# Another order for the loads of the first batch in a fused retention and mixer kernel, and halved copies of its half chunk

## Chip, core and metric

The kernel runs on one core of one Trainium2 chip. The metric is the device time in microseconds (us) from start to end of one execution; the time of a kernel is the median of its runs.

## What is computed

The inputs q, k, v have 8 batches, 8 heads, 576 positions and 64 features per head, float32. Stage one is a retention (attention without softmax and with a decay), stage two a low-rank mixing over the positions and then a two-layer network of width 2048:

```python
scores = scale * np.matmul(q, k.transpose(0, 1, 3, 2))
gamma = 1.0 - 2.0 ** (-5.0 - np.arange(H, dtype=np.float32))
Dmat = np.where(rel >= 0, gamma[:, None, None] ** rel[None, :, :], 0.0)
ret = np.matmul(scores * Dmat[None], v)          # then heads side by side: x
h = x.transpose(0, 2, 1) @ U @ V                 # U: 576 x 32, V: 32 x 576
u = x + h.transpose(0, 2, 1)
out = u + np.maximum(u @ w_ch1, 0.0) @ w_ch2     # 512 -> 2048 -> 512
```

## The kernel before, in words

Positions are cut into chunks of 128; a batch has four and a half of them, and two batches share one chunk (number 4, `XC`), each with one half of its 64 + 64 rows. I call that part of batch 0 or 1 the half chunk. The decay is split into a factor on q and one on v, so that within a chunk the scores are only masked (the product is called SC, the masked result `ret`), and what earlier chunks contribute is a running state S = k'v, kept in PSUM (ST) and multiplied by q (QS). RV multiplies `ret` by v into PSUM; the sum is copied to the tile x (L759 and L757 for pairs of chunks, L932 for a half chunk). MA multiplies U by x to a 32-row result a; `build` transposes x through the identity and adds V times a on PE, and copies the result to uT (L1041, L1043). Y1 is the first layer (weights w1, 64 products for each group of four chunks, ReLU on ScalarE), Y2 the second, added to u and stored.

Batches 0 and 1 have a path of their own, since nothing else can cover their loads. q of batch 0 comes in two transfers, k and v as pairs of chunks (`load_pair`, names k0, v0 for chunks 0 and 1, k2, v2 for chunks 2 and 3), the half chunk by `load` as kA, qA, vA for batch 0 and kB, qB, vB for batch 1. U comes in two transfers (lu), V in one (lv, L1164), which reads V's 32 rows four times over, to fill 128 partitions. The weights come in 16 transfers w0 to w15. All of these are issued on the SP queue. Casting and scaling are spread over GpSimd (POOL), VectorE (DVE) and ScalarE (ACT): k casts at L521 and L523, v scaled at L526 for pairs and at L472 for a half chunk, q of the half chunk at L478, U at L1169, V at L1173, V's second copy at L1177, weights at L1197 and L1215.

The order in which each engine works is fixed when the kernel is built. Every piece of work is an `Op` with engine, an assumed duration, dependences, buffers taken and given back, and a priority; `Plan.run` simulates the engines with these durations and picks, for each engine, the next op by time and priority. Its transfers share one ring: a transfer is done `work` after the one before it, plus `DMA_LAT`, and SP does not issue more than `DMA_AHEAD` ahead of the ring. The order of the first 40 or so loads is not left to it: a line of names is written out by hand and each load is put after the one before it (L1329 to L1331):

```python
line = [ld["q4a", 0], ld["q4", 0]] + [load_op(x) for x in ("k0 k2 v0 kA qA v2 vA lu lv w0 w1" + " " + "w2 w3 w4 w5 w6 w7 w8 w9 q4 w10 w11 kB k5 qB vB v5 k7 w12 w13 w14 w15 lub v7").split()]
for a, b in zip(line, line[1:]):
    b.after.append(a)
```

Before the first Y1 the planned gaps on PE are filled with products of a zero tile (`zeros`, from L1348), which have no use but to keep PE at work. The first three output tiles of Y1 are done in two halves, so that they can start when two of the four uT pieces and the first weight cast are ready.

Of the kernel before, what the change touches and what calls it, by code (L numbers as in the profile page):

```python
# [28 lines left out]
class Plan:  # L29

    LAT = {"PE": 230.0, "ACT": 80.0, "DVE": 80.0, "POOL": 90.0}
    LOOK = {"DVE": 150.0, "ACT": 150.0}
    DMA_LAT = 1700.0
    DMA_AHEAD = 4500.0

    def __init__(self):
        self.ops = []
# [21 lines left out]
    def run(self, hint=None):  # L59
        size = {name: len(x) for name, x in self.pools.items()}  # L60
        self.pools = {name: [0.0] * n for name, n in size.items()}
        self.held, self.spans, since = {}, {}, {}
        for o in self.ops:
            o.users, o.ready = [], 0.0
        urgent = {"DVE": [], "ACT": []}
        if hint:
            for o in self.ops:
                if o.prio < 0 and o.engs[0][0] in urgent and len(o.engs) == 1:
                    urgent[o.engs[0][0]].append(o)
        engines = ("PE", "ACT", "DVE", "POOL", "SP")  # L70
        free = dict.fromkeys(engines, 0.0)
        ring = 0.0
        avail = {e: [] for e in engines}
        for o in self.ops:
            o.n_wait = len(o.deps) + len(o.after)
            for d in o.deps + o.after:
                d.users.append(o)

        def add(o):
            pe = o.engs[0][0] == "PE"  # L80
            o.ready = max([d.end if pe and d.engs[0][0] == "PE" else d.vis for d in o.deps]
                          + [d.end for d in o.after], default=0.0)
            for e, dur in o.engs:
                avail[e].append((o, dur))

        for o in self.ops:
            if not o.n_wait:
                add(o)
        order = []
        left = len(self.ops)  # L90
        INF = float("inf")

        self.n_rel, self.last = {}, {}
        for o in self.ops:
            for x in o.rel:
                self.n_rel[x] = self.n_rel.get(x, 0) + 1
        for pool in self.line:
            self.line[pool] = sorted(
                (o for o in self.ops if any(x[0] == pool for x in o.acq)), key=lambda o: o.prio
            )  # L100

        def earliest(o):
            t = o.ready
            for pool, key in o.acq:
                if pool in self.line and self.line[pool][0] is not o:
                    return INF
                n = sum(x[0] == pool for x in o.acq)
                t = max(t, sorted(self.pools[pool])[n - 1])
            return t

        wary = bool(hint)
        while left:
            best = None
            for e in engines:
                base = free[e]
                if e == "SP":
                    base = max(base, ring - self.DMA_AHEAD)
                te = INF
                cand = []
                for o, dur in avail[e]:  # L120
                    t = max(base, earliest(o))
                    if t == INF:
                        continue
                    if wary and o.prio > 0 and any(
                        t < (max(hint[h], h.ready)) < t + dur - 150.0 for h in urgent.get(e, ())
                    ):
                        continue
                    cand.append((t, o, dur))
                    te = min(te, t)
                if te == INF:  # L130
# [12 lines left out]
            _, e, o, dur, t = best  # L143
            for en, _ in o.engs:
                avail[en] = [x for x in avail[en] if x[0] is not o]
            o.start, o.end = t, t + dur
            if hint and e in urgent and o in urgent[e]:
                urgent[e].remove(o)
            free[e] = o.end
            if e == "SP":  # L150
                ring = max(ring, t + 700.0) + o.work
                o.vis = ring + self.DMA_LAT
            elif o.work:
                ring = max(ring, o.end + 500.0) + o.work
                o.vis = ring + self.DMA_LAT
            else:
                o.vis = o.end + self.LAT[e]
            for pool, key in o.acq:
                if pool in self.line:
                    self.line[pool].pop(0)  # L160
                s = self.pools[pool]
                i = min(range(len(s)), key=lambda i: s[i])
                s[i] = INF
                self.held[pool, key] = i
                since[pool, key] = o.start
            for x in o.rel:
# [12 lines left out]
        return order  # L179
# [3 lines left out]
def kernel(  # L183
# [11 lines left out]
    nc = tc.nc  # L195
# [74 lines left out]
    def slot(pool, key):  # L270
        return pl.held[pool, key]
# [75 lines left out]
    def DMA(issue, work, fn, **kw):  # L347
        return pl.op("SP", issue, fn, work=work, **kw)
# [4 lines left out]
    def load_q4(par, prio):  # L353
# [5 lines left out]
        for n, hs in enumerate(halves):  # L359
            def fn(e, hs=hs):  # L360
# [2 lines left out]
                    out=q4.rearrange("p (h x) -> p h x", h=H)[:, hs, :],  # L363
                    in_=q[par, hs, t0:t0 + 4 * P, :].rearrange("h (p r) d -> p h (r d)", r=4),
                )
            gots.append(DMA(600.0, 3300.0 if par else (1500.0, 2400.0)[1 - n], fn, prio=prio + 0.01 * n,
                            acq=[] if n else keys))
        ld["q4", par] = gots[-1]
        ld["q4a", par] = gots[0]
# [57 lines left out]
    def load(p, c, prio, early=False, b=None):  # L427
# [17 lines left out]
        for n, (j, dram) in enumerate(((1, k), (0, q), (2, v))):  # L445

            def fn(e, j=j, dram=dram):
                f = at(j)
                for rw, bb, t0 in pts:
# [1 line left out]
                        out=f[rw, :, :],  # L451
                        in_=dram[bb, :, t0:t0 + rw.stop - rw.start, :].rearrange("h s d -> s h d"),
                    ))
            got[j] = DMA(480.0 if len(pts) == 1 else 900.0, 1220.0 if b is None else 1000.0, fn,
                         prio=prio + (0.0, 0.01, 0.5)[n], acq=[] if j == 2 else [home[j]],
                         after=[] if j == 1 else [got[1]])
            if p:
# [430 lines left out]
    def RV(p, c, prio, q_done=True, b=None, in_sc=False):  # L888
# [33 lines left out]
        def ev(e):  # L922
# [5 lines left out]
                ),  # L928
                op=ALU.mult,
            )  # L930
        def ev_x(e):
            nc.scalar.activation(out=xs[slot(*xk)][rows].rearrange("p hp hl d -> p hl hp d"),  # L932
                                 in_=po[rows, :, 0:NHP * D].rearrange("p hl (hp d) -> p hl hp d", d=D),
                                 func=AF.Copy)
        if b is None:
            st["x", kb] = [pl.op("DVE", 700.0, ev, [o], prio, rel=[pk])]
        else:
            st["x", kb] = [pl.op("ACT", 610.0, ev_x, [o], prio, rel=[pk])]
        if b is not None:
            st.setdefault(("x", c), []).extend(st["x", kb])  # L940

# [209 lines left out]
    def load_uv():  # L1151
# [11 lines left out]
        def fv(e):  # L1163
            nc.sync.dma_start(out=vst, in_=moe_V[None, :, :].to_broadcast([4, R, S]))  # L1164

        ld["lu"] = DMA(1200.0, 500.0, fu, prio=-999.0, after=[ld["consts"]])
        ld["lub"] = DMA(1200.0, 500.0, fub, prio=-999.0)
        ld["lv"] = DMA(500.0, 800.0, fv, prio=-999.0)
        ld["U"] = pl.op("POOL", 250.0, lambda e: gp.tensor_copy(out=UU[:, 0:5, :], in_=ust[:, 0:5, :]),  # L1169
                        [ld["lu"]], -970.0)  # L1170
        ld["UB"] = pl.op("POOL", 250.0, lambda e: gp.tensor_copy(out=UU[:, 5:10, :], in_=ust[:, 5:10, :]),
# [8 lines left out]
    def load_w(prio):  # L1180
        ld["lw"] = []
        for fb in range(4):
            ld["w1", fb] = []
            for hc in range(2):
                key = ("wst", ("w1", fb, hc))

                def fn(e, fb=fb, hc=hc, key=key):
# [3 lines left out]
                            "(c p) n -> p c n", p=P),  # L1191
                    ))
                o = DMA(450.0, 1400.0 + 350.0 * (fb < 2), fn, prio=prio + fb + hc * 0.1, acq=[key])
                ld["lw"].append(o)

                def cast(e, fb=fb, hc=hc, key=key):
# [4 lines left out]
        for fb in range(4):  # L1201
            ld["w2", fb] = []
            for hf in range(2):
# [3 lines left out]
                def fn(e, f=f, key=key):  # L1207
                    sent.append(nc.sync.dma_start(
                        out=wst[slot(*key)].rearrange("p (f d) -> p f d", d=dm),
                        in_=moe_w_ch2[f * P:(f + 2) * P, :].rearrange("(f p) d -> p f d", p=P)))  # L1210
                o = DMA(450.0, 1400.0, fn, prio=prio + 10 + fb + hf * 0.1, acq=[key])
                ld["lw"].append(o)

                def cast(e, f=f, key=key):
# [9 lines left out]
    def batch0():  # L1224
# [2 lines left out]
        load_q4(0, base - 3.0)  # L1227
        t_q4(0, base - 2.0, 10.0)
        for i in range(2):
            load_pair(0, i, base + 20 * i, scaled=(2, 2)[i])  # L1230
        load(0, XC, base + 40.0, early=True, b=0)
        for r in range(4):
            t_pe(0, r, base + 10 * r + 2)
            SC_pair(0, r, base + 10 * r + 3, home=("po", "sc")[r % 2])
        t_pe(0, XC, base + 42.0, b=0)
        SC(0, XC, base + 43.0, with_q=False, b=0, apart="sc" == "big")
        sp = -4.0
        ST_four([base + sp, base + sp + 2, base + sp + 4, base + 5.0, base + 52.7])
        for i in range(2):
# [83 lines left out]
    def load_op(x):  # L1323
# [2 lines left out]
        if x[0] == "w":  # L1326
            return ld["lw"][int(x[1:])]
        return ld["q4", 1] if x == "q4" else L(x)[0]
    line = [ld["q4a", 0], ld["q4", 0]] + [load_op(x) for x in ("k0 k2 v0 kA qA v2 vA lu lv w0 w1" + " " + "w2 w3 w4 w5 w6 w7 w8 w9 q4 w10 w11 kB k5 qB vB v5 k7 w12 w13 w14 w15 lub v7").split()]  # L1329
    for a, b in zip(line, line[1:]):  # L1330
        b.after.append(a)  # L1331
    def shift(g):
# [67 lines left out]
```

## Time and profile before

| | |
|---|---|
| median of 6 runs | 337.85 us (336.59 to 340.07) |
| the profiled execution | 336.59 us, of which the span of the profile is 334.4 us |
| PE busy | 326.2 us of the span, 98% |
| DVE, ACT, POOL busy | 151.4, 134.6, 84.2 us |
| queue of SP's transfers (q1) | 47.12 MB, 69.3% of the 16 engines' span |
| first Y1 product | at 24.33 us |
| PE busy from 60 to 140 us | 79.99 of 80 us |

All times in the views count from the start of the span. A line of the chain of waits has start, length and what the time went to; in the lists in order of time a line has start, length, engine, line of the kernel, operation, output and input, count, and in square brackets the idle time before it with what ended it. A row of stretches gives, after the stretch's bounds, its length and the busy time of PE, PE's weight loads, DVE, ACT and POOL with their instruction counts, then the granted PE clock, the share of time in which the DMA engines were busy and the GB/s that they moved.

The loads up to w0 were issued at these times: k0 and k2 from 1.84, v0 3.46, kA 6.08, qA 7.81, v2 8.71, vA 9.57, U 11.46 and 12.28, V 13.51, w0 and w1 from 14.21 us.

### The profile page before, as it was taken

The page shows a single profiled execution, that of the slowest core. Times are in us where ns is not written, and L with a number is a line of the kernel's source. Part 1 is how long each engine was busy: PE and PEld are TensorE (multiplying, and loading weights), DVE is VectorE, ACT ScalarE, POOL GpSimd, SP SyncE. Part 2 cuts the span into 40 slices and gives each one's busy share as a digit, 9 for nine tenths or more (in the row PEclk, how much of TensorE's full clock was granted, in tenths as well). Part 3 has the DMA queues.
Part 4 walks back from the last instruction along what each step waited for, and adds up shares of the span by engine and source line. Part 5 has one row for each costly group of instructions (what it writes and reads, how often), then busy time and mean ns, then how long its engine had stood idle before and what let it go on. Part 6 is the DMA issues. An engine that isn't in the chain of part 4 may idle for free.

```text
span 334.4 us, 6464 instructions
## 1 busy us (share of the span) xinstructions
PE 326.2 (98%) x2656; PEld 161.0 (48%) x2656; DVE 151.4 (45%) x238; ACT 134.6 (40%) x240; POOL 84.2 (25%) x116
## 2 busy tenths in 40 slices
PE   8989999999999999999999999999999999999995
PEld 3554445555545544544454455444544444444442
DVE  5842275786555537664476538533633020020011
ACT  4756564478303650265114521364035206404600
POOL 7567456522321312131122113200100010010010
PEclk9999999999999999999999999999999999999999
DMA  8999999999999999999999989913110320011012
GB/s 238 228 305 359 296 247 301 266 244 187 192 257 207 226 179 213 233 221 205 185 235 227 188 186 235 217 37 49 63 65 16 71 89 31 0 65 63 0 51 76
DMA packets 145169, 56.44 MB, mean 169 GB/s; under 512 B 128244, under 2 KB 138484, under 8 KB 145140
## 3 DMA queue, kind: packets, MB, share of 16 engines
q1 hardware_dynamic: 142420, 47.12, 69.3%
q0 software_dynamic: 2720, 8.92, 7.7%
q8 instruction: 21, 0.34, 0.4%
q14 instruction: 8, 0.07, 0.1%
HBM read 37.14 MB, written 9.44 MB: 139 GB/s over the span
## 4 chain that ended last, share of the span: by engine, by line
PE 86%; DMA 8%; DVE 3%; POOL 1%; SPq 1%; issue 0%; DVEq 0%
PE ps_big_t L326 72%; DMA st_st<-in_k_dram 5%; PE ps_o L326 5%; PE ps_s L326 5%; PE ps_sc L326 3%; DMA vst<-in_moe_V_dram 2%; PE ps_big_t L566 1%; DVE ret_t L713 1%; DVE ret_t L857 1%; DVE o_sb L1127 0%; SPq L1156 0%; SPq L450 0%; POOL w_sb L1197 0%; PE ps_sc L401 0%; DVE qkv_t L468 0%
## 5 line engine op out<-in xcount | busy, mean ns | idle before, releaser
L326 PE MATMUL ps_big_t<-uT_t,w_sb 128*128 128x512 bf16 x576 | 133.7, 379 | 0.5 <-POOL w_sb L1197 0.5
L326 PE MATMUL ps_big_t<-w_sb,y_t 128*128 128x512 bf16 x576 | 133.3, 379 | 0.1
L1060 ACT ACTIVATE y_t<-ps_big_t 128x512 bf16<-128x512 f32 x144 | 85.8, 597 | 94.3 <-PE ps_big_t L326 94.1
L326 PEld LDWEIGHTS <-w_sb 128*128 128x128 bf16 x576 | 53.9, 98 | 62.1 <-POOL w_sb L1197 1.0
L326 PEld LDWEIGHTS <-y_t 128*128 128x128 bf16 x576 | 53.8, 98 | 60.9 <-issue 0.8
L1127 DVE TENSOR_TENSOR o_sb<-ps_big_t,u_t 128x512 f32<-128x512 f32 x36 | 24.7, 689 | 87.8 <-PE ps_big_t L326 87.7
L1134 POOL DMA_DIRECT2D out_dram<-o_sb x34 | 19.3, 567 | 161.6 <-DVE o_sb L1127 161.4
L472 POOL TENSOR_TENSOR qkv_t<-st_st,vscale 128x512 bf16<-128x512 f32 (+1 forms) x28 | 29.2, 1041 | 57.3 <-DMA st_st<-in_v_dram 43.1
L857 DVE TENSOR_TENSOR ret_t<-ps_sc,tri 128x1024 bf16<-128x1024 f32 x24 | 29.3, 1221 | 20.3 <-PE ps_sc L326 20.1
L798 ACT ACTIVATE s_sb<-ps_s 128x512 bf16<-128x512 f32 x22 | 13.1, 596 | 56.5 <-PE ps_s L326 56.4
L923 DVE TENSOR_TENSOR x_t<-ps_o,qscale 128x512 bf16<-128x512 f32 x27 | 18.6, 687 | 15.4 <-PE ps_o L326 15.3
L991 DVE TENSOR_TENSOR u_t<-ps_s,x_t 128x512 bf16<-128x512 f32 x20 | 13.8, 690 | 21.1 <-PE ps_s L326 21.0
L326 PEld LDWEIGHTS <-qkT_t 64*128 64x128 bf16 (+3 forms) x612 | 15.3, 99 | 11.0 <-issue 8.0
L326 PEld LDWEIGHTS <-ret_t 128*128 128x128 bf16 (+2 forms) x384 | 12.5, 99 | 8.2 <-issue 0.8
L468 DVE CAST qkv_t<-st_st 128x512 bf16<-128x512 f32 x27 | 13.6, 503 | 3.5 <-DMA st_st<-in_k_dram 3.5
L468 DVE CAST qkv_t<-q_st 128x512 bf16<-128x512 f32 x27 | 13.9, 516 | 2.3 <-DMA q_st<-in_q_dram 2.3
L326 PE MATMUL ps_o<-qkv_t,ret_t 128*128 128x64 bf16 (+2 forms) x344 | 13.2, 193 | 0.6 <-DVE ret_t L713 0.4
L326 PE MATMUL ps_sc<-qkT_t 64*128 64x128 bf16 (+2 forms) x336 | 13.3, 215 | 0.4 <-DVE ret_t L857 0.4
L326 PE MATMUL ps_s<-qkv_t 64*64 64x64 bf16 (+3 forms) x200 | 12.8, 207 | 0.5 <-issue 0.3
L326 PEld LDWEIGHTS <-qkv_t 64*64 64x64 bf16 (+3 forms) x232 | 9.9, 104 | 6.5 <-issue 2.8
L991 DVE TENSOR_TENSOR u_t<-ps_o,x_t 128x512 bf16<-128x512 f32 x16 | 10.9, 683 | 3.4 <-PE ps_o L326 3.3
L575 ACT ACTIVATE qkT_t<-ps_big_t 128x512 bf16<-128x512 bf16 (+1 forms) x21 | 10.9, 555 | 2.0 <-PE ps_big_t L566 1.7
(101 smaller groups left out, 178.7 us busy)
## 6 DMA issues: line engine op xcount, KB each, us to landing
out_dram<-o_sb POOLq DMA_DIRECT2D x34, 256.0 KB, 3.2
st_st<-in_k_dram SPq DMA_DIRECT2D x24, 256.0 KB, 4.6
q_st<-in_q_dram SPq DMA_DIRECT2D x24, 256.0 KB, 4.6
st_st<-in_v_dram SPq DMA_DIRECT2D x24, 256.0 KB, 5.2
y_t<-in_moe_w_ch_dram SPq DMA_DIRECT2D x10, 512.0 KB, 9.9
wst_t<-in_moe_w_ch_dram SPq DMA_DIRECT2D x6, 512.0 KB, 6.6
st_st<-in_k_dram SPq DMA_DIRECT2D x4, 512.0 KB, 7.5
st_st<-in_v_dram SPq DMA_DIRECT2D x4, 512.0 KB, 7.8
```

The lines of the kernel that those rows point to most:

```text
L326: nc.tensor.matmul(*a, skip_group_check=True, **kw)
L468: nc.vector.tensor_copy(**args)
L472: eng.tensor_tensor(out=qkv[slot(*qk)][rows, 2, :, :], in0=at(2)[rows], in1=vscale[rows, c, :, None].to_broadcast([rows.stop - rows.start, ...
L566: nc.tensor.transpose(pst()[:, hp, :], t[rows, j, 2 * hp:2 * hp + 2, :].rearrange("p h d -> p (h d)"), ident[rows, rows],)
L575: nc.scalar.activation(func=AF.Copy, **args)
L798: nc.scalar.activation(out=s_sb[slot(*sk)], in_=ps_s.rearrange("p (a b) -> p a b", b=P), func=AF.Copy)
L857: nc.vector.tensor_tensor(out=ret[slot(*rk)][rows, hl, :, 0:n], in0=bank(hl.start)[rows, None, :, 0:n] if apart else ps_sc[rows, hl, :, 0: ...
L923: nc.vector.tensor_tensor(out=xs[slot(*xk)][rows].rearrange("p hp hl d -> p hl hp d"), in0=po[rows, :, 0:NHP * D].rearrange("p hl (hp d) - ...
L991: nc.vector.tensor_tensor(out=us[slot(*uk)].rearrange("p (hp hl d) -> p hp hl d", hl=2, d=D), in0=bank().rearrange("p (hp hl d) -> p hp hl ...
L1060: nc.scalar.activation(out=y1s[slot(*yk)][:, f, :], in_=ps_big[slot(*bk)], func=AF.Relu)
L1127: nc.vector.tensor_tensor(out=osb[slot(*ok)], in0=ps_big[slot(*bk)], in1=osb[slot(*ok)] if n else us[slot(*uk)], op=ALU.add)
L1134: eng.dma_start(out=out_flat[row:row + P, :], in_=osb[slot(*ok)])
```

## The change

The loads of batch 0 go k0, v0, k2, v2, kA, qA, U, V, vA instead of k0, k2, v0, kA, qA, v2, vA, U, V. The copy of the half chunk's x from PSUM becomes two copies of half the size, one on ACT and one on DVE, in batches 0 and 1. The planner's assumptions on transfers change: `DMA_LAT`, a few `work` and issue times, and a rule of its own (`RING`) for how far SP runs ahead, which holds for all loads but the weights in the first 60 us. Apart from the halved copies, a few casts that change engine and fewer zero products in one place and more in another, the instructions stay the same; the order on the engines changes where the planner's times led it to.

In the order on POOL, the scaling of vA (L472) moves from before U's cast to behind V's second copy (L1177), ahead of the first weight cast. On PE the products with k2 and k3 come later, the state products of chunks 0 and 1 earlier; fewer zero products stand in between. The cast of kB moves from ACT to POOL. Some loads of the shared chunk of batches 2 and 3 are issued earlier, and a few groups of products of batches 1 to 3 change places.

```diff
-    DMA_LAT = 1700.0
+    DMA_LAT = 2100.0
     DMA_AHEAD = 4500.0
+    RING = 2900.0
...
-                if e == "SP":
-                    base = max(base, ring - self.DMA_AHEAD)
...
                     t = max(base, earliest(o))
+                    if e == "SP":
+                        t = max(t, ring - self.DMA_AHEAD if o.name == "w" or ring > 60000.0 else ring + o.work - dur - self.RING)
...
-        def ev_x(e):
-            nc.scalar.activation(out=xs[slot(*xk)][rows].rearrange("p hp hl d -> p hl hp d"),
-                                 in_=po[rows, :, 0:NHP * D].rearrange("p hl (hp d) -> p hl hp d", d=D),
-                                 func=AF.Copy)
+        def ev_x(e, hl, insts):
+            args = dict(out=xs[slot(*xk)][rows, :, hl, :],
+                        in_=po[rows, hl, 0:NHP * D].rearrange("p (hp d) -> p hp d", d=D))
+            insts.append(nc.scalar.activation(func=AF.Copy, **args) if e == "ACT" else nc.vector.tensor_copy(**args))
+            if len(insts) == 2:
+                own(insts)
...
-            st["x", kb] = [pl.op("ACT", 610.0, ev_x, [o], prio, rel=[pk])]
+            insts = []
+            st["x", kb] = [pl.op(e, 390.0, lambda e, hl=hl: ev_x(e, hl, insts), [o], prio, rel=[pk])
+                           for hl, e in enumerate(("ACT", "DVE"))]
...
-        ld["lu"] = DMA(1200.0, 500.0, fu, prio=-999.0, after=[ld["consts"]])
+        ld["lu"] = DMA(1300.0, 500.0, fu, prio=-999.0, after=[ld["consts"]])
...
-        ld["lv"] = DMA(500.0, 800.0, fv, prio=-999.0)
+        ld["lv"] = DMA(660.0, 800.0, fv, prio=-999.0)
...
-    line = [ld["q4a", 0], ld["q4", 0]] + [load_op(x) for x in ("k0 k2 v0 kA qA v2 vA lu lv w0 w1" + " " + "w2 w3 w4 w5 w6 w7 w8 w9 q4 w10 w11 kB k5 qB vB v5 k7 w12 w13 w14 w15 lub v7").split()]
+    line = [ld["q4a", 0], ld["q4", 0]] + [load_op(x) for x in ("k0 v0 k2 v2 kA qA lu lv vA w0 w1" + " " + "w2 w3 w4 w5 w6 w7 w8 w9 q4 w10 w11 kB k5 qB vB v5 k7 w12 w13 w14 w15 lub v7").split()]
```

More of the change, by code (lines that the diff above doesn't have):

```diff
@@ L365, in fn @@
                 )
-            gots.append(DMA(600.0, 3300.0 if par else (1500.0, 2400.0)[1 - n], fn, prio=prio + 0.01 * n,
+            gots.append(DMA(600.0, 3300.0 if par else (1300.0, 2200.0)[1 - n], fn, prio=prio + 0.01 * n,
                             acq=[] if n else keys))
@@ L453, in fn @@
                     ))
-            got[j] = DMA(480.0 if len(pts) == 1 else 900.0, 1220.0 if b is None else 1000.0, fn,
+            got[j] = DMA(480.0 if len(pts) == 1 else 900.0, 1220.0 if b is None else 1250.0, fn,
                          prio=prio + (0.0, 0.01, 0.5)[n], acq=[] if j == 2 else [home[j]],
@@ L1193, in load_w @@
                 o = DMA(450.0, 1400.0 + 350.0 * (fb < 2), fn, prio=prio + fb + hc * 0.1, acq=[key])
+                o.name = "w"
                 ld["lw"].append(o)
@@ L1211, in load_w @@
                 o = DMA(450.0, 1400.0, fn, prio=prio + 10 + fb + hf * 0.1, acq=[key])
+                o.name = "w"
                 ld["lw"].append(o)
@@ L1229, in batch0 @@
         for i in range(2):
-            load_pair(0, i, base + 20 * i, scaled=(2, 2)[i])
+            load_pair(0, i, base + 20 * i, scaled=2)
         load(0, XC, base + 40.0, early=True, b=0)
@@ L1235, in batch0 @@
         t_pe(0, XC, base + 42.0, b=0)
-        SC(0, XC, base + 43.0, with_q=False, b=0, apart="sc" == "big")
+        SC(0, XC, base + 43.0, with_q=False, b=0)
         sp = -4.0
```

## The prediction

> **What bounds the kernel now.** I read the page first, then the stretches with busy times by engine, then the chain of waits, then POOL and TensorE (PE) in order of time.
>
> ```profile
> PE 326.2 (98%) x2656; PEld 161.0 (48%) x2656; DVE 151.4 (45%) x238; ACT 134.6 (40%) x240; POOL 84.2 (25%) x116
> ```
>
> PE is busy for 98% of the span, but the first part of that is filler products on the zero tile. The stretches show where time could still be won or lost:
>
> ```profile
> 20.00:28.00 8.00, 6.98 (x51) 3.39 (x48) 2.90 (x5) 4.23 (x8) 5.43 (x6) 1.00 1.04 356
> 34.00:46.00 12.00, 11.66 (x71) 5.71 (x70) 5.79 (x11) 6.84 (x14) 4.69 (x6) 1.00 1.08 254
> 46.00:60.00 14.00, 12.84 (x224) 7.21 (x223) 9.44 (x11) 5.95 (x11) 9.11 (x10) 1.00 1.09 293
> 60.00:140.00 80.00, 79.99 (x712) 41.12 (x706) 48.47 (x77) 34.65 (x61) 21.05 (x25) 1.00 1.11 220
> ```
>
> The first pair of numbers is length and PE busy time. From 60 us on PE has no idle time, between 34 and 60 us it lacks 0.34 + 1.16 = 1.5 us. So the end is set by when the first product of the two large layers (Y1) starts, 24.33 us, and by at most 1.5 us of idle behind it. The chain of waits says what sets that start:
>
> ```profile
> 13.51 8.33 DMA vst<-in_moe_V_dram
> 21.83 0.05 issue
> 21.89 0.68 POOL VV L1173
> 22.56 0.05 issue
> 22.62 0.67 POOL VV L1177
> 23.28 1.00 POOL w_sb L1197
> 24.28 0.05 issue
> 24.33 1.68 PE ps_big_t L326 x7
> ```
>
> (Columns: start, length, what.) V's transfer takes 8.33 us from issue to landing, then POOL casts V, copies it, and only then casts the first weights. The change goes for this transfer. What it moves to make room is the half chunk's v, so I look at that too:
>
> ```profile
> 17.82 1.04 POOL L472 TENSOR_TENSOR qkv_t<-st_st,vscale 64x512 bf16<-64x512 f32 x1 [0.26 <-DMA st_st<-in_v_dram]
> 18.80 0.31 POOL L1169 CAST UU<-ust 128x160 bf16<-128x160 f32 x1
> 21.89 0.67 POOL L1173 CAST VV<-vst 128x576 bf16<-128x576 f32 x1 [2.77 <-DMA vst<-in_moe_V_dram]
> 22.62 0.67 POOL L1177 COPY VV<-VV 128x576 bf16<-128x576 bf16 x1
> 23.23 2.10 POOL L1197 CAST w_sb<-wst_t 128x1024 bf16<-128x1024 f32 x2
> ```
>
> ```profile
> 19.68 0.43 PE L326 MATMUL ps_sc<-qkv_t,ret_t 64*64 64x64 bf16 x8
> ...
> 21.16 0.37 PE L326 MATMUL ps_big_t<-x_t,UU 64*32 64x512 bf16 x1 [0.19 <-ACT x_t L932]
> ...
> 22.61 0.59 PE L326 MATMUL ps_big_t<-VV,a_sb 128*128 128x512 bf16 x2 [0.35 <-POOL VV L1173]
> ```
>
> The half chunk's v lands at 17.77, POOL scales it by 18.86, and PE's product of it (RV of the half chunk, 19.68) begins a chain that also ends at Y1: x, U times x, a, V times a, the copies to uT. That chain waits only 0.35 us for V. Two chains thus arrive almost together, and the change takes from one and gives to the other.
>
> **V's transfer, moved ahead of the half chunk's v.** In the trace's semaphore events V's transfer is counted up by four engines only, at 20.50, 20.93, 21.18 and 21.83; every other input is counted by sixteen. Those four engines had finished U by 17.05 at the latest, so 32 packets of 2304 B took some 4.5 to 4.8 us on each. The first weight load, issued after V, landed on most engines by 18.8 but on the last four at 21.96, 22.28, 22.35 and 22.94, 1.1 to 1.5 us after each completion of V: it stood behind V there. The row against which I hold a rule is the 8.33 us. The Trainium skill (DMA: Bandwidth & Descriptors, "Why a DMA increments its semaphore by 16 and not by 1") says that a transfer runs on the largest number of engines up to 16 that divides the slowest dimension of both sides, the lowest-numbered ones; V is read as [4, 32, 576], so 4, as the trace counts, while the half chunk's v has 64 on both sides and needs all 16. Its "Queues, rings and completion order" adds that each engine takes its descriptors in ring order. Reckoned by bytes instead, 288 KB at the 372 GB/s of the stretch 21 to 26 us are 0.8 us, and v would lose next to nothing by standing behind V. By the row and this rule, it is complete only when its shares on V's four engines have followed V, 4 us later than today. I take the row.
>
> How early does V land? It is moved ahead of v's packets, whose share per engine I take from completions: the second v pair completes at a median of 15.1, the half chunk's v at 16.1, so 1.0 us. V lands at 21.83 - 1.0 = 20.85, its casts run 20.90 to 21.6 and (start to start 0.73 as in the rows) 21.63 to 22.3. The half chunk's v lands 0.7 to 1.0 us behind V, at 21.5 to 21.85.
>
> **POOL's order.** In the changed kernel's order POOL has U's cast, V's cast, V's copy, and only then the scaling of the half chunk's v, then the weights. So that scaling waits for both: it starts at 22.25 (0.61 after the copy, as L1197 does now) and ends at 23.29. Queued behind it: both first weight casts, which end at 24.3 and 25.3, as now. Who waits: RV of the half chunk on PE, at 23.33 instead of 19.68, and all of PE's order behind it.
>
> **From there to Y1.** With today's steps: RV and state term 0.84 (19.68 to 20.52), copying out x in halves 0.43 (DVE's 64x256 cast at 18.47; today one 0.59 on ACT, so the split gains 0.16), 0.05 to PE, U times x 0.41, a 0.60, 0.05, V times a 0.69 until the second copy may begin, DVE's copy 0.69, 0.05: 3.81 us. 23.33 + 3.81 = 27.14, against 24.33: **+2.8 us**. The wait for V (0.35) and for the weight cast (0.48) are gone; v is what is late next.
>
> **The pairs' new order.** k, v, k, v instead of k, k, v: the first v lands where the second k did (about 9.8), the second k where the first v did (about 12), so the third and fourth masks on DVE (13.09, 14.22 now) run some 2 us later, and with the interleaved copies the second RV pair ends near 18.6 and PE's last work before the half chunk near 19.6. Cost nothing: covered by the wait until 23.33. Without that cover it would cost up to about 1 us (second RV pair is at 18.44 now).
>
> **Behind Y1.** Weight casts 3 and later still follow their landings, so the loads of batch 1 keep their times and PE comes to them 2.8 us later. Of PE's four gaps there (0.25, 0.39, 0.41, 0.34 us) the first ends with the landing of batch 1's k at 45.03 and goes; the others end on DVE masks or PE's own order, which shift along. Gain 0.3; bounds 0.2 and 1.5 (all idle). The other edits (batch 1's x in halves, its half chunk's k cast on POOL instead of ACT, some loads of batches 2 and 3 and a few matmul groups in another order) lie behind Y1's start, mostly where PE has no idle time to give back; I put them at 0, with a bound of 0.5 either way. The larger planner constants are in no instruction.
>
> Sum: +2.8 - 0.3 = +2.5 us. On the profiled execution (span 334.4, time 336.59) that is 339.1; that run is the fastest of six, and on their median of 337.85 it is **340.4 us**. A measurement can tell about 0.5% (1.7 us) from no change.
>
> **Rivals.**
> 1. The clock drops. PE would be idle from about 19.6 to 23.3, 3.7 us. At the end of the trace PE stops at 330.5 and the granted clock falls within 333.8:334.4 (0.54 there), after about 3.3 us of idle; the first 14 filler products take 0.40 us each, later ones about 0.22. The skill (TensorE: Matmul & The Clock Gate, Part 1) has free-running windows of 3.4 us, so by an estimate from it 3.7 us of idle hold a whole window only about one time in ten; by the 3.3 us alone the clock would always drop. I lie between, nearer the rule. If it does, PE's pieces of the chain (about 1.3 us) double, and up to 3.4 us of Y1 go at half rate: +1 to +3, 341.4 to 343.4. Chance 0.15.
> 2. All the idle is absorbed: PE comes so late that batch 1's data, masks and copies are ready. 1.5 instead of 0.3 goes: +1.3, 339.2, within 0.5%. Against it: three of the four gaps end on work that PE itself starts. Chance 0.15.
> 3. The other side, not slower: V's four engines go faster. In its stretch (16.5 to 21 us) the core moves 241 GB/s against 372 after, and a 2304 B packet takes 150 ns; at the later rate V takes 3.1 us, lands near 19.2, v is scaled by 21.7, Y1 starts at 25.5: +1.2 - 0.3 = +0.9, 338.8. It decides if V lands before 19.6, where the sum falls below 0.5%. Against it: the same weights are loaded beside it as now. Chance 0.12.
> 4. v is not held up, and only V is earlier. Then the first weight load (22.94) sets the cast at 24.0 and Y1 at 24.05: -0.3; with all later idle, -1.8. Against: POOL's order alone forbids it. Chance 0.05.
>
> The forecast itself has 0.53, with 339.6 to 341.2. Faster by over 0.5% 0.03, within 0.27, slower 0.70. The range 338.2 to 343.0 takes in rivals 2 and 3 and most of 1.
>
> **What would show it.** Right: in the profile after, POOL's scaling of the half chunk's v starts past 22 us, directly behind the copy of V; PE idles 3 us or more before the first 64x64 product into ps_sc with ret_t; Y1 starts near 27. Wrong: V landing before 19.6, that scaling standing at 18 us, or the time from 60 us on no longer filled by PE.

## The result

The changed kernel has a median of 341.99 us (338.25 to 344.07, 37 runs) against 338.15 us of before on the same chip (335.53 to 341.49, 74 runs). The ratio is 1.0096 with a 95% interval of 1.008 to 1.0112, so the change makes the kernel slower by about 1%, 3.2 us by the ratio and 3.8 by the medians; 2.5 had been forecast. The ratio leaves out runs more than 1.5% above the fastest of the same kernel, which the medians include.

The median lies within the stated range of 338.2 to 343.0, but not within the 339.6 to 341.2 of the forecast itself. It lies where the first rival, the fallen clock, had put it (341.4 to 343.4).

### The profile page after: what moved, and what is told of

It is laid out like the page before. It is cut to its first block, busy times and chain, and to the rows that moved or that the text cites. A ratio compares the mean times of both kernels' runs of the same rounds, so it can differ in the third digit from the quotient of the medians.

```text
span 339.1 us, 6471 instructions
## 1 busy us (share of the span) xinstructions
PE 328.2 (97%) x2656; PEld 161.7 (48%) x2656; DVE 154.5 (46%) x241; ACT 132.7 (39%) x238; POOL 85.1 (25%) x117
## 4 chain that ended last, share of the span: by engine, by line
PE 90%; SPq 3%; DMA 3%; DVE 1%; POOL 1%; issue 0%; ACT 0%; DVEq 0%
PE ps_big_t L327 75%; PE ps_o L327 5%; PE ps_s L327 5%; PE ps_sc L327 4%; DMA vst<-in_moe_V_dram 3%; SPq L509 2%; PE ps_big_t L567 1%; SPq L451 1%; DVE ret_t L714 0%; ACT qkT_t L576 0%; SPq L1161 0%; POOL qkv_t L473 0%; SPq L363 0%; PE ps_sc L402 0%; SPq L1160 0%
## 5 line engine op out<-in xcount | busy, mean ns | idle before, releaser
L327 PE MATMUL ps_big_t<-uT_t,w_sb 128*128 128x512 bf16 x576 | 133.6, 379 | 0.0
L327 PE MATMUL ps_big_t<-w_sb,y_t 128*128 128x512 bf16 x576 | 133.1, 379 | 0.0
L327 PEld LDWEIGHTS <-w_sb 128*128 128x128 bf16 x576 | 53.9, 98 | 61.2 <-issue 1.3
L327 PEld LDWEIGHTS <-y_t 128*128 128x128 bf16 x576 | 53.8, 98 | 60.9 <-issue 0.7
L473 POOL TENSOR_TENSOR qkv_t<-st_st,vscale 128x512 bf16<-128x512 f32 (+1 forms) x28 | 29.3, 1047 | 54.2 <-DMA st_st<-in_v_dram 39.3
L924 DVE TENSOR_TENSOR x_t<-ps_o,qscale 128x512 bf16<-128x512 f32 x27 | 18.6, 688 | 16.7 <-PE ps_o L327 16.6
L327 PEld LDWEIGHTS <-qkT_t 64*128 64x128 bf16 (+3 forms) x612 | 15.3, 99 | 9.9 <-issue 7.2
L327 PEld LDWEIGHTS <-ret_t 128*128 128x128 bf16 (+2 forms) x384 | 12.7, 99 | 10.5 <-issue 3.3
L469 DVE CAST qkv_t<-st_st 128x512 bf16<-128x512 f32 x27 | 15.4, 570 | 0.9 <-DMA st_st<-in_k_dram 0.9
L327 PE MATMUL ps_o<-qkv_t,ret_t 128*128 128x64 bf16 (+2 forms) x344 | 13.2, 193 | 0.9 <-ACT qkT_t L576 0.9
L327 PE MATMUL ps_sc<-qkT_t 64*128 64x128 bf16 (+2 forms) x336 | 13.3, 215 | 0.4 <-DVE ret_t L858 0.4
L327 PE MATMUL ps_s<-qkv_t 64*64 64x64 bf16 (+3 forms) x200 | 12.4, 207 | 0.7 <-POOL qkv_t L527 0.6
L327 PEld LDWEIGHTS <-qkv_t 64*64 64x64 bf16 (+3 forms) x232 | 9.7, 104 | 7.1 <-issue 3.3
```

Of the source, the lines that this page charges most:

```text
L327: nc.tensor.matmul(*a, skip_group_check=True, **kw)
L469: nc.vector.tensor_copy(**args)
L473: eng.tensor_tensor(out=qkv[slot(*qk)][rows, 2, :, :], in0=at(2)[rows], in1=vscale[rows, c, :, None].to_broadcast([rows.stop - rows.start, ...
L924: nc.vector.tensor_tensor(out=xs[slot(*xk)][rows].rearrange("p hp hl d -> p hl hp d"), in0=po[rows, :, 0:NHP * D].rearrange("p hl (hp d) - ...
```

## The profile after

The profiled execution took 340.79 us, its span is 339.1 us (before: 334.4). All lines of the changed kernel stand a little further down in its text than before: L473 scales the half chunk's v (L472 before), L1178 casts V (L1173), L1182 copies it (L1177), L1203 casts weights (L1197), L327 holds the matmuls (L326).

The total first, then PE's waits (line, what ended the wait, total us, times, longest):

```profile
PE 328.2 (97%) x2656; PEld 161.7 (48%) x2656; DVE 154.5 (46%) x241; ACT 132.7 (39%) x238; POOL 85.1 (25%) x117
```

```profile
PE ps_sc L327 <- POOL qkv_t L473: 2.2, 1, 2.2
...
PE ps_o L327 <- ACT qkT_t L576: 0.9, 1, 0.9
PE ps_s L327 <- POOL qkv_t L527: 0.6, 1, 0.6
```

The greatest wait of PE is a new one, for the scaled v of the half chunk. The waits for V's cast and for the weights' cast that before had are gone. The chain of waits names the same transfer as before, but goes on along another way:

```profile
12.53 8.58 DMA vst<-in_moe_V_dram
21.11 0.05 issue
21.16 0.68 POOL VV L1178
21.84 0.05 issue
21.89 0.67 POOL VV L1182
22.56 1.01 POOL qkv_t L473
23.57 0.04 issue
23.61 0.78 PE ps_sc L327 x16
...
29.15 2.68 PE ps_big_t L327 x12
```

V, cast, copy, then the scaling of v in place of the weight cast. Y1 starts at 28.99 instead of 24.33 us (the 29.15 of the chain is where this piece of it starts). POOL and PE in order of time:

```profile
17.63 0.32 POOL L1174 CAST UU<-ust 128x160 bf16<-128x160 f32 x1 [0.86 <-DMA ust<-in_moe_U_dram]
21.16 0.67 POOL L1178 CAST VV<-vst 128x576 bf16<-128x576 f32 x1 [3.21 <-DMA vst<-in_moe_V_dram]
21.89 0.67 POOL L1182 COPY VV<-VV 128x576 bf16<-128x576 bf16 x1
22.52 1.04 POOL L473 TENSOR_TENSOR qkv_t<-st_st,vscale 64x512 bf16<-64x512 f32 x1
23.51 2.01 POOL L1203 CAST w_sb<-wst_t 128x1024 bf16<-128x1024 f32 x2
```

```profile
21.09 0.29 PE L327 MATMUL ps_big_t<-ident,x_t 128*128 128x128 bf16 x2
23.61 0.41 PE L327 MATMUL ps_sc<-qkv_t,ret_t 64*64 64x64 bf16 x8 [2.24 <-POOL qkv_t L473]
...
27.39 1.06 PE L327 MATMUL ps_big_t<-VV,a_sb 128*128 128x512 bf16 x2
...
28.99 2.20 PE L327 MATMUL ps_big_t<-uT_t,w_sb 128*128 128x512 bf16 x9
```

V times a took 0.59 us before and takes 1.06 here, the same two products of the same shape. The stretches say why. I cut them along the grid on which the granted clock changes in the trace, every 3.413 us (the fields are those of the tables before: length, PE busy, ..., clock, DMA share, GB/s):

```profile
18.20:21.61 3.41, 2.71 (x58) 1.77 (x55) 2.13 (x4) 1.39 (x3) 0.45 (x1) 1.00 1.06 253
21.61:25.02 3.41, 1.41 (x19) 0.90 (x18) 0.42 (x1) 0.38 (x1) 3.35 (x5) 1.00 1.05 386
25.02:28.43 3.41, 3.41 (x17) 1.76 (x17) 0.00 (x0) 0.97 (x2) 2.78 (x4) 0.50 1.05 387
28.43:31.84 3.41, 3.41 (x17) 1.46 (x15) 1.89 (x3) 1.65 (x4) 2.85 (x3) 1.00 1.04 366
```

In the second of these PE was busy for 1.41 of 3.41 us; the third ran at half the clock although PE was at work all through it. This is the first rival, to which I had given 0.15. A fallen clock is not an accident of this one execution, though only this one shows where it fell. One such stretch lowers a run's mean granted clock by 0.005 (half the clock for 3.41 of 339 us); of the 38 runs of the changed kernel whose clock is known six have a mean clock of 0.997 or more (median 339.0 us), fourteen 0.993 to 0.995 (341.4) and eighteen 0.984 to 0.990 (342.6). In the four sets of before's runs beside the experiments 4 of 51, 5 of 51, 9 of 51 and 5 of 27 have 0.995 or less.

What lies behind Y1 became shorter by the 0.3 us forecast, but not in the way forecast. From Y1 to PE's last product it is 330.50 - 24.33 = 306.17 us before and 334.85 - 28.99 = 305.86 after. PE's idle time in it fell only from 1.67 to 1.56 us: the gaps of 0.25, 0.41 and 0.34 us that before had are gone, and a new one is there, for the transposed q and k (`qkT_t`) of batch 1:

```profile
56.65 0.64 PE L327 MATMUL ps_o<-qkv_t,ret_t 64*128 64x64 bf16 x32 [0.94 <-ACT qkT_t L576]
```

That the sum comes out at 0.3 is luck.

```profile
46.00:60.00 14.00, 12.47 (x225) 7.49 (x223) 10.18 (x15) 7.77 (x17) 8.47 (x9) 1.00 1.03 270
60.00:140.00 80.00, 79.97 (x695) 40.67 (x688) 49.68 (x76) 33.99 (x60) 21.46 (x25) 1.00 1.06 214
```

PE still has no idle time from 60 us on, so the later start is paid in full.

## The experiments

The theory: the half chunk's v, behind V on V's four engines and behind V's casts on POOL, starts the chain to Y1 late. Rival theories: the fallen clock is the larger part; the pairs' new order costs by itself; the planner's constants cost by what they make of the order elsewhere. They were timed in four sets, each beside the kernel before on one chip, so ratios are compared across sets and medians only within one. "Clock" gives the runs whose mean granted clock is 0.995 or less; the others I call runs with an unfallen clock. "Y1 at" comes from the one profiled execution of each kernel; line numbers are each kernel's own.

| kernel | median, before | ratio (95%) | clock | Y1 at |
|---|---|---|---|---|
| changed kernel | 341.99, 338.15 | 1.0096 (1.008 to 1.0112) | 32 of 38 | 28.99 |
| e2_only_v_behind | 342.64, 337.77 | 1.0151 (1.0107 to 1.0195) | 6 of 6 | 27.39 |
| e10_v_behind_filler | 340.38, 338.11 | 1.0071 (1.0046 to 1.0095) | 4 of 22 | 27.46 |
| e4_filler | 339.78, 337.77 | 1.0091 (1.0065 to 1.0118) | 1 of 15 | 27.26 |
| e3_v16 | 340.29, 337.77 | 1.0057 (1.003 to 1.0084) | 5 of 21 | 26.61 |
| e1_v_ahead_again | 340.66, 337.77 | 1.0079 (1.0052 to 1.0105) | 12 of 22 | 26.11 |
| e5_pairs_only | 341.59, 338.0 | 1.0068 (1.004 to 1.0097) | 15 of 22 | 26.85 |
| e7_planner_only | 340.35, 338.0 | 1.0059 (1.0034 to 1.0084) | 11 of 22 | 26.29 |
| e8_halves_only | 338.33, 338.0 | 1.0001 (0.997 to 1.0032) | 5 of 14 | 24.38 |
| e9_v_ahead_chunk_order | 341.72, 338.0 | 1.0104 (1.0054 to 1.0153) | 6 of 6 | 28.34 |
| e12_clean_undo | 339.51, 338.11 | 1.0041 (1.0013 to 1.0069) | 3 of 22 | 26.21 |
| e14_clean_undo_bare | 338.77, 337.44 | 1.0025 (1.0001 to 1.0049) | 7 of 22 | 26.45 |
| e6_v16_before | 338.48, 338.11 | 1.0013 (0.9978 to 1.0048) | 1 of 14 | 22.84 |

### The swap alone, without and with the clock held

The kernel before with one name moved:

```diff
-... k0 k2 v0 kA qA v2 vA lu lv w0 ...
+... k0 k2 v0 kA qA v2 lu lv vA w0 ...
```

> The kernel before with one edit: the half chunk's v issued behind U and V. Theory: POOL's scaling of it starts near 22.5, RV of the half chunk near 23.6, Y1 at 27.4 to 29 depending on the granted clock, and the time is 0.7 to 1.1% above before, as the whole change. Rival (pair order or planner): within 0.3% of before.

```profile
20.97 0.67 POOL L1173 CAST VV<-vst 128x576 bf16<-128x576 f32 x1 [2.61 <-DMA vst<-in_moe_V_dram]
21.70 0.67 POOL L1177 COPY VV<-VV 128x576 bf16<-128x576 bf16 x1
22.33 1.04 POOL L472 TENSOR_TENSOR qkv_t<-st_st,vscale 64x512 bf16<-64x512 f32 x1
```

These are the rows of the changed kernel, 0.2 us earlier, and RV of the half chunk starts at 23.42 after 2.08 us of idle. So the swap alone makes the late start. In all six runs the clock fell as well. Only the profiled one shows where, and there it was at another place, behind the idle time at 53 to 56.5 us (of which 0.58 us is a stop within one group of products that no wait explains):

```profile
53.12:56.53 3.41, 2.35 (x90) 1.85 (x88) 2.67 (x3) 2.75 (x5) 2.85 (x3) 1.00 1.11 327
56.53:59.94 3.41, 3.29 (x41) 1.95 (x35) 1.90 (x2) 1.19 (x2) 2.21 (x4) 0.50 0.99 216
```

To part the two I put nine products of the zero tile on PE, just ahead of that RV, into its wait:

```diff
         for o, e in order:
+            if o.name == "RVX":
+                for _ in range(9):
+                    mm(ps_s, zer[:, 0:P], zer, start=True, stop=True)
```

> The order of before with one name moved: the half chunk's v behind U and V, as in e2_only_v_behind (1.0151 there, Y1 at 27.39 us), and nine zero products on PE just ahead of the half chunk's RV, so that PE is not idle for 2 us before it. Theory (the late v costs about 2 us by itself and the fallen clock the rest): Y1 stays at 27.2 to 27.6 us, the mean granted clock is 0.997 or more in most runs, and the ratio to before is 1.006 to 1.010. Rival (the clock is an accompaniment, and the late start alone is worth the 1.5%): the ratio stays at 1.013 or more. Second rival (PE's idle time is harmless and only the clock costs): the ratio is within 0.2% of 1.

```profile
21.20 2.12 PE L326 MATMUL ps_s<-zer 128*128 128x512 bf16 x9
23.49 0.41 PE L326 MATMUL ps_sc<-qkv_t,ret_t 64*64 64x64 bf16 x8 [0.18 <-POOL qkv_t L472]
```

The first theory came in. RV stands at 23.49 and Y1 at 27.46, nearly as in the kernel without these products, and the ratio falls from 1.0151 to 1.0071; the intervals do not meet. Of the 18 runs with an unfallen clock the median is 340.02, against 337.75 for such runs of before: +2.3 us is what the late v costs by itself. The rest of the 1.5%, up to 2.7 us, came with the clock. The same products in the changed kernel:

> The changed kernel with nine more products of the zero tile on PE right ahead of the half chunk's RV, where PE now waits 2.24 us. They leave every dependence as it is. Theory (v's lateness costs about 3 us of Y1's start, and the clock that falls at 25.02 for 3.41 us another 1.6): RV still at 23.6, the clock stays at full rate, Y1 starts near 27.3 instead of 28.99, and the time falls by 1.5 to 2 us, leaving about 0.4 to 0.5% over before. Rival (the clock fell for another reason, or is not what lengthened the chain): time as the changed kernel, within 0.2%.

```profile
21.61:25.02 3.41, 3.41 (x31) 1.75 (x29) 0.42 (x1) 0.38 (x1) 3.37 (x5) 1.00 1.05 387
25.02:28.43 3.41, 3.41 (x22) 1.52 (x20) 1.55 (x3) 1.79 (x3) 2.81 (x3) 1.00 1.05 374
```

The clock stays at 1.00 (one run in 15 lower, where the changed kernel has 32 in 38), Y1 starts at 27.26 where 27.14 was forecast for an unfallen clock, and the median is 2.0 us above its own before, where the changed kernel's is 3.8 above. But its ratio, 1.0091, has an interval that covers the changed kernel's (the medians give 1.006; why the two differ is not known), so that by this pair alone the clock's price is not shown; the pair before shows it.

### V on sixteen engines

The changed kernel with V as four transfers of its 32 rows:

```diff
-            nc.sync.dma_start(out=vst, in_=moe_V[None, :, :].to_broadcast([4, R, S]))
+            for i in range(4):
+                nc.sync.dma_start(out=vst[32 * i:32 * i + 32, :], in_=moe_V)
```

> The changed kernel, but V is read by four transfers of 32 rows each instead of one transfer that repeats the 32 rows four times, so that each can be spread over sixteen engines. Theory (only four engines carry V, and v stands behind it there): V lands near 17, v near 18, both weights earlier than 22.9; v is scaled by 20.5; RV of the half chunk follows PE's own order near 21.4, Y1 near 25.2; time 0.9% under the changed kernel or more, about before. Rival (order alone, or bytes moved, holds v up): V still lands after 20, time unchanged. Against both: three more issues on SP, some 0.65 us each, ahead of v and the weights.

```profile
18.86 0.67 POOL L1179 CAST VV<-vst 128x576 bf16<-128x576 f32 x1 [0.67 <-DMA vst<-in_moe_V_dram]
19.59 0.67 POOL L1183 COPY VV<-VV 128x576 bf16<-128x576 bf16 x1
21.52 1.04 POOL L473 TENSOR_TENSOR qkv_t<-st_st,vscale 64x512 bf16<-64x512 f32 x1 [1.26 <-DMA st_st<-in_v_dram]
```

Each quarter was now counted by sixteen engines within 0.2 to 0.3 us, and the last one landed at 18.71 instead of 21.11. So the four engines were what made V slow, and the number of bytes was not. The four issues take SP 3.1 us, so the half chunk's v was issued at 17.28 only (changed kernel: 13.23). It landed by 20.15 on fifteen engines and at 21.45 on the last, 4.2 us after its issue instead of 8.2: the group of four engines that came 2.7 us behind the rest is gone. Why one engine was still late is not shown.

The other expectations failed. v was complete no earlier than in the changed kernel (21.43 there), the first weight landed at 23.0, RV stands at 22.61, 1.0 us earlier than in the changed kernel but not near 21.4, Y1 at 26.61, not 25.2, and the time fell by 0.4%, not by 0.9. An earlier v would have gained little more, since PE's own work before RV ended at 22.53.

### Undoing parts

The changed kernel with the half chunk's v put back ahead of U and V. I expected the time of before:

```diff
-... k0 v0 k2 v2 kA qA lu lv vA w0 ...
+... k0 v0 k2 v2 kA qA vA lu lv w0 ...
```

> The changed kernel, only with the half chunk's v issued ahead of U and V again; pair order, halved copies and planner constants stay. Theory (v held up behind V's four engines, then behind V's casts on POOL): v is scaled by 18, RV of the half chunk no longer waits, Y1 starts near 24.5 instead of 28.99, no idle of 2 us on PE, and the time falls by about 3 us to within 0.3% of the kernel before. Rival (the pairs' order, which makes the second pair's masks 2 us later, or the planner's new order later on is what costs): the time stays over 0.6% above before.

This failed, and the time is where the rival had it. v is scaled at 16.67, but Y1 starts at 26.11 only, and the clock falls in half of the runs. Part of it is in the first 26 us: RV stands at 22.07, behind the second RV pair, which runs at half the clock. Part of it is later:

```profile
68.20 0.40 PE L567 MATMUL ps_big_t<-ident,qkv_t 128*128 128x128 bf16 x4 [0.83 <-DVE qkv_t L469]
...
70.83 0.62 PE L567 MATMUL ps_big_t<-ident,qkv_t 128*128 128x128 bf16 x8 [0.71 <-DVE qkv_t L469]
72.02 0.39 PE L327 MATMUL ps_o<-a_sb,VV 128*128 128x512 bf16 x1 [0.58 <-DVE uT_t L1048]
```

q of batch 2 lands at 70.3 there, because the planner's new rule puts eight transfers of shared chunks, 128 KB each, ahead of it. In the changed kernel PE comes later and does not meet this wait. So I took the other parts one by one. First the pairs' order alone, in before:

```diff
-... k0 k2 v0 kA qA v2 vA lu lv w0 ...
+... k0 v0 k2 v2 kA qA vA lu lv w0 ...
```

> The kernel before with one edit: k0, v0, k2, v2, kA, qA, vA, U, V. Theory (three separate costs: v behind V, the pairs' order, and loads of batch 2 that the planner pulls forward): the second pair's masks run 2 us later, RV of the half chunk stands near 21.2 instead of 19.68, Y1 starts near 25.2, no idle between 60 and 75 us, time 0.2 to 0.5% above before, more if the clock falls as it did in the run with v ahead again. Rival (only v behind V costs): within 0.2% of before.

It costs 0.68% by the ratio and 1.06% by the medians; its seven runs with an unfallen clock have a median of 339.32 against 337.73 for such runs of before, +1.6 us. The rival is out. The fourth mask runs at 18.75 (before: 14.22), the second RV pair at 21.21, and the clock fell in 15 of 22 runs. In this execution the first k was also late on one engine (9.54 us; 8.03 in the changed kernel's profile), so its start does not stand for the median. Then the planner's constants and rule alone (with the small `work` and issue times that the change's diff shows), and the halved copies alone:

```diff
-    DMA_LAT = 1700.0
+    DMA_LAT = 2100.0
+    RING = 2900.0
```

> The changed kernel's planner constants and RING rule, with the line of loads and the whole copy of the half chunk's x as before. Theory: Y1 starts as before, near 24.3, but SP issues eight 64-row transfers of the shared chunks at 50 us ahead of batch 2's first chunk, PE idles 1.5 to 2.5 us in the transposes of batch 2 between 65 and 75 us, and the time is 0.5 to 0.8% above before. Rival (the order of these loads is without effect, as the prediction had it): within 0.2%.

```diff
-            st["x", kb] = [pl.op("ACT", 610.0, ev_x, [o], prio, rel=[pk])]
+            st["x", kb] = [pl.op(e, 390.0, lambda e, hl=hl: ev_x(e, hl, insts), [o], prio, rel=[pk])
+                           for hl, e in enumerate(("ACT", "DVE"))]
```

> The kernel before with the half chunk's x copied in two halves, nothing else. All theories: RV to U times x is shorter by 0.1 to 0.2 us, the time is within 0.2% of before.

The halves show no cost (the interval reaches 0.3% to either side). The planner's part costs 0.59%, and not where I had expected it: between 60 and 80 us PE idles 0.57 us. One thing that it did was to move V's cast from POOL to DVE, ahead of a copy of x on which PE waits:

```profile
22.42 0.46 DVE L1175 CAST VV<-vst 128x576 bf16<-128x576 f32 x1 [1.31 <-DMA vst<-in_moe_V_dram]
22.91 0.69 DVE L760 CAST x_t<-ps_o 128x512 bf16<-128x512 f32 x1
```

```profile
23.66 0.38 PE L327 MATMUL ps_big_t<-x_t,UU 128*32 128x512 bf16 x1 [0.73 <-DVE x_t L760]
```

DVE works in order, so the copy, whose input PE had ready at 21.71, stands behind a cast whose input landed at 22.40. But this wait is not shown to be the 0.59%: in this execution RV was already at 21.64, 2.0 us later than before, and from RV to Y1 it took 4.65 us in both kernels. The first v pair was late on one engine here (13.44 us; 12.18 before), so what makes RV late in the median stays open. The next kernel is the one with v ahead again and the later batches' shared loads held back:

```diff
+            if p and c == XC:
+                got[j].after.append(ld["v", (p, 3)])
```

> The run with v ahead again, with one more edit: the loads of the shared chunk of later batches may not be issued before the fourth chunk of their own batch, which restores before's order of loads from batch 2 on. Theory: the idle time of 2.1 us between 67 and 72 us is gone, and the time falls by 0.5 to 0.6% against that run, to 0.1 to 0.4% above before (what is left is the pairs' order). Rival (something else at 67 us): idle and time as in that run.

PE has no idle time left between 60 and 80 us (20.00 of 20), as meant, but the time did not fall. One loss is again V's cast, which stands on ACT ahead of x.

```profile
23.89 0.68 ACT L1182 ACTIVATE VV<-vst 128x576 bf16<-128x576 f32 x1 [2.41 <-DMA vst<-in_moe_V_dram]
24.48 0.58 ACT L760 ACTIVATE x_t<-ps_o 128x512 bf16<-128x512 f32 x1
```

PE waits 0.93 us for that x, and the clock fell in all six runs. In the profiled one the first k was late on one engine (9.85 us), PE waited 1.72 us for its cast, and the clock fell at 12 us, so this profile can't say what the other five lost. So I also kept V's cast on POOL behind the scaling of v, with and without the nine zero products:

```diff
-        ld["V"] = pl.op("ACT", 680.0, lambda e: (...), [ld["lv"]], -935.0, alt=[("DVE", 600.0), ("POOL", 700.0)])
+        ld["V"] = pl.op("POOL", 700.0, lambda e: (...), [ld["lv"]], -935.0)
...
+        ld["V"].after.append(st["v", (XC, 0)])
```

> The changed kernel with everything undone that was found to cost on this path: the half chunk's v ahead of U and V, its scaling ahead of V's cast on POOL (the cast is kept on POOL), the shared chunk's loads of later batches not before their batch's fourth chunk, and nine zero products before the half chunk's RV to hold the clock. What is left of the change is k, v, k, v, the halved copies and the planner's order elsewhere. Theory (the pairs' order is free when the clock holds, and the three others explain the change's cost): Y1 at 24.3 to 25.2 us, clock 0.997 or more in most runs, ratio 0.998 to 1.003. Rival (k, v, k, v costs by itself, by the later masks and the later second RV pair): Y1 at 25.5 to 26.5 us and a ratio of 1.004 to 1.007.

> As e12_clean_undo, without its nine zero products. There they were the delay: PE had the second RV pair done at 20.3 us and the half chunk's v was scaled by 19.0, and the zero products held PE until 22.2, so that Y1 started at 26.2 and the ratio was 1.0041. Theory (k, v, k, v costs nothing here, since V lands later than the half chunk's chain needs it): the half chunk's RV starts at 20.3 to 20.5 us instead of 19.68, Y1 at 24.5 to 25.0, set by V's landing and the casts behind it as in before; PE idles about 1 us for V; the clock is 0.995 or less in a quarter of the runs at most; ratio 0.998 to 1.003. Rival (something else of the change costs 0.4%, and the zero products did not matter): the ratio stays at 1.004 or above with Y1 before 25 us, and the trace has idle time of PE behind 30 us that before does not have.

In the first Y1 (26.21) and the ratio came out as the rival had them, but the zero products were themselves the delay, since nothing was left to wait for (v was scaled by 18.99):

```profile
20.19 2.11 PE L327 MATMUL ps_s<-zer 128*128 128x512 bf16 x9
22.23 0.43 PE L327 MATMUL ps_sc<-qkv_t,ret_t 64*64 64x64 bf16 x8
```

Without them 1.0025 is left, inside what the theory gave. Its profiled execution shows Y1 at 26.45, not the 24.5 to 25.0 I expected, as the clock fell at 19.4 us in it, behind a stop of 0.97 us within the first RV pair that no wait explains; in the 15 of 22 runs without that the median is 337.92, against 337.28 of such runs of before, +0.6 us. So with v ahead, V's cast kept out of x's way and the later loads in order, the remains of the change (k, v, k, v, the halves and the planner's order elsewhere) cost 0.25%, with an interval that begins at 0.01%.

### A version meant to be faster

The kernel before with the edit of e3_v16 alone:

> The kernel before, whose loads keep their order, but V comes as four transfers of its 32 rows, each of which can run on all sixteen engines, in place of one that runs on four. Theory (V's casts and the first weight cast bound Y1 together with the half chunk's chain): V is complete by 18.5 us instead of 21.8, its cast starts at 18.9 behind the scaling of the half chunk's v, and Y1 starts at 23.4 to 23.7 us instead of 24.33, set by the half chunk's chain; ratio 0.997 to 0.999. Rival (the three further issues on SP push the first weights 2 us later and these set Y1): Y1 at 24.3 us or later and a ratio of 1.000 to 1.004.

Y1 starts at 22.84, 1.5 us earlier than before and earlier than either theory had it, and loses it at once:

```profile
22.84 1.61 PE L326 MATMUL ps_big_t<-uT_t,w_sb 128*128 128x512 bf16 x6
26.19 1.47 PE L326 MATMUL ps_big_t<-uT_t,w_sb 128*128 128x512 bf16 x6 [1.74 <-POOL w_sb L1198]
```

PE waits 1.74 us for the second weight, whose cast begins with its landing, at 25.09 us. The rival had the right cause and the wrong weight. That weight, w1, was issued at 17.53 instead of 14.69. Of these 2.8 us, 2.0 are the three further issues and the rest a wait of SP: the loads take eight semaphores (counters of landings) in turn, and w1 came to the one of the half chunk's v, which landed at 17.52. The ratio is 1.0013 and shows no gain.

## Why the prediction was right, point by point

- **V on four engines, v behind it: right.** V's completions are at 20.52, 20.69, 20.83 and 21.11 (20.85 forecast). The half chunk's v was counted by twelve engines at 16.58 to 18.47 and by the last four at 21.16, 21.33, 21.35 and 21.43 (21.5 to 21.85 forecast). e3_v16 shows the cause by taking it away: v's time from issue to landing falls from 8.2 to 4.2 us. The rule of the Trainium skill that I weighed there (DMA: Bandwidth & Descriptors, "Why a DMA increments its semaphore by 16 and not by 1") is borne out on both sides: four engines for V as [4, 32, 576], sixteen for 32 rows.
- **POOL's order: right.** Scaling 22.52 (22.25), RV 23.61 (23.33).
- **3.81 us from RV to Y1: the term that was mis-sized.** It took 5.38. With the clock held it is 27.26 - 23.23 = 4.03 in e4_filler and 27.46 - 23.49 = 3.97 in e10_v_behind_filler, so 0.2 of the 1.57 more are the sum's own error and 1.4 the half-rate stretch from 25.02 us. The step stands, and what failed was rival 1's chance of 0.15: I counted on a whole window without work, while a window in which PE was busy for 41% was enough.
- **Idle of 3.7 us from 19.6: too long.** PE idled 2.24, since its last work ended at 21.37; the 3 us or more that were to show the prediction right did not come. The masks came at 14.81 and 17.14, 1.7 and 2.9 us later than before, and the second RV pair started at 19.64, while I had it end near 18.6. Even without the late v, PE would have come to RV 1.69 us later than before (21.37 instead of 19.68); v made it 3.93.
- **The pairs' order at nothing, up to 1 us without its cover: a size too small.** Alone it costs 0.68% (2.3 us, the clock included), and 1.6 us in its runs with an unfallen clock.
- **The planner's constants "in no instruction": wrong as a reason.** They set the order, and in before's line of loads they cost 0.59%. In the changed kernel itself V's cast is on POOL, and PE comes late enough to miss the wait at 67 us, so neither of these two waits is seen there. The parts of the change cost by turns, not in sum: alone 1.51, 0.68 and 0.59%, together 0.96%.
- **0.3 absorbed behind Y1: right in number, by luck.** The gap that was to go (0.25) went, but so did two others, and a new one of 0.94 us took their place. Rival 2, with all idle absorbed, did not come.
- **Rivals 3 and 4: excluded.** V did not land before 19.6, and v was held up.

So the mechanism was right, and +2.5 us fits the late start where the clock is held: +2.3 in e10_v_behind_filler and, by its runs with an unfallen clock, 339.75 - 337.48 = 2.3 in e4_filler. The rest to 3.2 or 3.8 us would then be the clock. How the two share the cost within the changed kernel is not settled: its own six runs with an unfallen clock have a median of 339.0, only 0.9 us above before's 338.15. They may be the runs in which the wait for v was short, but no trace of them shows it.

Left open besides: how much of the 0.25% of e14_clean_undo_bare is the later masks; what makes e7_planner_only slow; and what, beside PE's idle time, makes the clock fall.

## What to carry to other kernels

Before a load is moved, count on how many engines each transfer completes in the trace: one that runs on few engines can hold up a later one that needs them all by more than its bytes suggest (here by 2.7 us, where 0.8 us had been reckoned by bytes). Follow the moved load's consumer on its in-order engine too, where it may stand behind a cast of data that is later still. And price new idle time of PE by more than its length: a wait of some 2 us in front of a chain of products can be followed by 3.4 us at half the clock, and zero products in the wait made that rarer (4 of 22 runs instead of 6 of 6, 1 of 15 instead of 32 of 38). They have to end before the data are there.

## What the runs showed of the hardware

- **Half a stretch of idle time is enough for the clock to fall, but does not always do it.** Along the 3.413 us grid of the 14 profiles, PE was busy less than half of a stretch twice (41 and 49%), and the clock fell both times; between 50 and 60% five times, and it fell twice; between 60 and 80% 27 times, and it fell twice (74% in e1_v_ahead_again, 69% in e2_only_v_behind); above 80% it never fell. The fall lasted one stretch each time. In three of the six stretches before a fall PE had stopped for 0.58 to 0.97 us within a group of products, waiting for nothing that the profile shows. The Trainium skill (TensorE: Matmul & The Clock Gate, Part 1) speaks of an idle window; here windows with work in them were enough, and the measurement decides.
- **One DMA engine can be late at the start.** The first k was complete on all engines at 8.03 us in the changed kernel, at 9.54 in e5_pairs_only and at 9.85 in e9_v_ahead_chunk_order. Single profiles of the first 30 us can therefore differ by 1.5 us or more, and only medians of runs tell such kernels apart.
